# Attention and mixture of experts on one core: head parity of q and K on alternate partitions, W1 from tile 2 on

## The chip, the cores and the metric

The kernel runs on one core of a Trainium2 chip. The metric is the device time of one execution in microseconds. A profile of one execution comes with the runs; its times are read from the start of its span.

## What is computed

Eight batches of 576 tokens with eight heads of 64 go through attention in chunks of 64 tokens; the result, 4608 rows of 512, goes through a layer of eight experts. Each row either skips the layer or goes to the one expert with the highest logit.

```python
scores = scale * np.matmul(q_c, k_c.transpose(0, 1, 2, 4, 3))      # chunks of 64
scores = scores - np.max(scores, axis=-1, keepdims=True)
attn = np.exp(scores); attn = attn / (attn.sum(-1, keepdims=True) + 1e-09)
x = heads_to_rows(np.matmul(attn, v_c))                            # 4608 x 512
do_compute = x @ w_skip > 0
e_idx, gate_w = argmax and softmax weight of x @ w_gate
h = np.maximum(x @ w1[e], 0.0)                                     # 512 -> 1024
out = x + do_compute * gate_w * (h @ w2[e])                        # 1024 -> 512
```

## The kernel before

**Two parts.** The first part walks over 36 tiles of 128 tokens (two chunks) and does the attention, the router's logits and, spread over the tiles, the routing. The second part takes the experts one after the other in an order found at run time, gathers the rows of each, and multiplies them with W1 (`hp`, L483) and W2 (`sp`, L508). The order of the instructions on each engine is the order in which the Python code writes them.

**A tile of the first part.** Four loads bring it in: q (one transfer, L133), K (two, L136) and v (one, L141), all on SP's queue. A tile of q or K has 128 rows of 512 floats: the contraction index, head dimension by parity of the head, lies on the partitions, so two heads share a tile of 128 partitions. K's tile `kbd` is twice as wide, with the heads of parity 0 in the left half on one half of the partitions and those of parity 1 in the right half on the other; the rest is zero. One matmul so gives the scores of two heads apart (`pe_scores`, L240). There are six K tiles, filled with zeros once at the start (L147) and used in turn. The first of K's transfers goes to partitions 0 to 63, the second to 64 to 127.

Then come, each on its engine: the copy of the scores out of PSUM on ACT (`sc`, L245), the row maximum on DVE (L250), its subtraction on POOL (L255), the exponential on ACT (`px`, L259), the transpose on PE (L266) and its copy on ACT (`ps`, L271), the product with v on PE (L279), the division on DVE (`x`, L292), another transpose (L307) and the split into two float16 halves (L312, L317) for the logits (L324). The loop in line 675 runs these for neighbouring tiles in one iteration: scores of tile i, exponential and transpose of tile i-1, the product with v of tile i-2, and so on. Tile i+5's q and K and tile i+4's v are asked for in iteration i.

**The first expert's weights.** Beside the tiles the weights of the expert that comes first are loaded and split into float16 halves, in 16 pieces: eight of W1, then eight of W2. `W_AT` lists the tile at which each piece is asked for (`load_piece`, L351). Near the end of an iteration one piece may be converted: `conv_w1` (L357 on ACT, L358 on DVE) for W1, `scale_w2` and `conv_w2` (L362, L363 on ACT, L367 on POOL) for W2, when the tile number is at least two above the piece's entry in `W_AT` (L710, L712). The pieces share four buffers `wst`. On ACT a conversion so stands between the `ps` copy of one tile and the `sc` copy of the next.

**Stores.** The x of a tile is stored by SP (L301), from tile `X_FROM` on one a tile, towards the end three. Gathers of rows for the first expert (POOL, L227) read them back, the first ones late in the first part.

**The start.** DVE fills the first two K tiles, POOL the other four, each half tile by itself; then DVE makes the constants `ones` and `zeros`, with which PE runs ten warm-up matmuls (L171) ahead of the first scores.

Of the kernel before, what the change touches and what calls it, by code (L numbers as in the profile page):

```python
# [18 lines left out]
P = 128  # L19
B, H, S, D = 8, 8, 576, 64  # L20
CH = 64
NTOK = B * S
NT = NTOK // P
DM = H * D
NE = 8
FF = 1024
KC = DM // P
FC = FF // P
# [8 lines left out]
WSETS = 3  # L37
PACE, PACE1 = 2800.0, 1500.0
QB, KB, VB, AHEAD, VAHEAD = 6, 6, 6, 5, 4
W_AT = tuple(range(1, 9)) + tuple(range(10, 34, 3))  # L40
X_FROM = 9
XB = 14
TLEAD = 2
LLEAD = 1
# [34 lines left out]
def constants():  # L79
    c, r = np.zeros((P, CCOLS), np.float32), np.zeros((1, RCOLS), np.float32)  # L80

    def put(name, a):
        lo, hi = (_C if name in _C else _R)[name]
        (c if name in _C else r)[:, lo:hi] = np.asarray(a, np.float32).reshape(-1, hi - lo)

    put("ident", np.eye(P))
    put("upper", np.triu(np.ones((P, P)), 1))
    put("wdesc", np.arange(NE, -1, -1))
    put("cbase", np.tile([*(np.arange(NE) * RS), NE * RS - RS // 2], GS[0]))
    put("cb8", -RS * np.arange(NE))  # L90
    put("last", np.arange(P)[:, None] * np.ones(P) == P - 1)
    put("tri", np.tril(np.ones((NE, NE))))
    put("kbase", np.arange(NE)[::-1] - NE * RS * np.arange(NE) + (1 << 19) * (np.arange(NE) == FIRST))
    put("eio", np.arange(NE))
    put("eio2", np.repeat(np.arange(NE), NE))
    put("caps", np.repeat([sum(b) for b in BLOCKS], NE))
    put("jthr", P * np.arange(NJ))
    put("siota", np.arange(NJ))
    tok = np.arange(NT)[None, :] * P + np.arange(P)[:, None]
    put("tok", tok)  # L100
    put("tlo", tok % TB + 1)
    put("thi", tok // TB)
    put("iota", np.arange(P))
    put("cell", RS * np.arange(NE)[:, None] + P * np.arange(NB)[None, :])
    return c, r
# [3 lines left out]
def moe_attention_kernel(ctx: ExitStack, tc: tile.TileContext, qk: bass.AP, vv: bass.AP, cst: bass.AP, crow: bass.AP, wall: bass.AP, out: bass.AP):  # L109
    nc = tc.nc  # L110
# [15 lines left out]
    T = [dict() for _ in range(NT)]  # L126
    halves = (slice(0, CH), slice(CH, P))
    kbd = [ap.tile([P, 2, DM], F32, name=f"k{i}", bufs=1) for i in range(KB)]

    def load_qk(t):  # L130
        if t < NT:
            T[t]["q"] = ap.tile([P, DM], F32, name="q", bufs=QB)
            nc.sync.dma_start(T[t]["q"], qk[t, 0])  # L133
            T[t]["k"] = kbd[t % KB]
            for a, r in enumerate(halves):
                nc.sync.dma_start(T[t]["k"][r, a], qk[t, 1, r])  # L136

    def load_v(t):
        if t < NT:
            T[t]["v"] = ap.tile([P, 2, KC, VW], F32, name="v", bufs=VB)  # L140
            nc.sync.dma_start(T[t]["v"], vv[t])  # L141
# [1 line left out]
    man = tc.manual_schedule()  # L143
    man.__enter__()
    for i, k in enumerate(kbd):
        for a, r in enumerate(halves):
            (nc.vector if i < 2 else nc.gpsimd).memset(k[r, 1 - a], 0.0)  # L147
    csb = cpool.tile([P, CCOLS], F32, name="csb")
    rsb = cpool.tile([1, RCOLS], F32, name="rsb")
    load_qk(0)  # L150
    nc.sync.dma_start(csb, cst)
    load_qk(1)
# [40 lines left out]
    def more_constants():  # L193
        w = C("wsg").rearrange("p (k n) -> p k n", k=KC)
        nc.vector.tensor_scalar(wsg[:, :, 0], w, SW, None, op0=ALU.mult)
        nc.vector.scalar_tensor_tensor(wsg[:, :, 1], w, SW, wsg[:, :, 0], op0=ALU.mult, op1=ALU.subtract)

        nc.vector.tensor_copy(iota, C("iota").unsqueeze(2).to_broadcast([P, P, G]))

    def route_constants():  # L200
        nc.gpsimd.tensor_copy(upper, C("upper"))
        nc.gpsimd.tensor_copy(cbase, C("cbase"))
        nc.gpsimd.tensor_copy(recs[:, :, 0], C("tok"))
        nc.gpsimd.tensor_copy(rvs[:, :, 0], C("tlo"))
        nc.gpsimd.tensor_copy(rvs[:, :, 1], C("thi"))
# [92 lines left out]
    def store_x(n):  # L298
        for _ in range(min(n, len(xq))):
            t, x = xq.pop(0)  # L300
            nc.sync.dma_start(out[t * P:(t + 1) * P, :], x)  # L301
# [28 lines left out]
    def route_step():  # L330
        c = next(routes[0][1], None)
        if c is None:
            done_g.append(routes.pop(0)[0])
        paused[0] = c is LATE
        return c or 0.0

    def route_late():
        if paused[0]:
            route_step()

    cws, cw2, stw, done1 = [], [], [None], [0]

    def load_piece(m):
        kind, f = m // FC, m % FC
        r = slice(kind * P * KC, (kind + 1) * P * KC)
        if not kind or f % 2 == 0:
            while len(cws) + len(cw2) // 2 >= STB:
                conv_w1()
            stw[0] = stpool.tile([P, CW], F32, name="wst")
        st = stw[0][:, DM * (kind * f % 2):][:, :DM]  # L350
        nc.sync.dma_start(st, wall[FIRST, f, :, r])  # L351
        (cw2 if kind else cws).append((st, wsets[0][:, 0, f, r], wsets[0][:, 1, f, r]))

    def conv_w1():
        st, hi, lo = cws.pop(0)
        done1[0] += 1
        nc.scalar.activation(hi, st, AF.Copy, scale=SW)  # L357
        nc.vector.scalar_tensor_tensor(lo, st, SW, hi, op0=ALU.mult, op1=ALU.subtract)  # L358
# [253 lines left out]
    def on(f, t):  # L612
        if 0 <= t < NT:
            f(t)
# [32 lines left out]
    scaled, done2 = [0], [0]  # L647

    def more_w2(n):
        for m in range(done2[0], min(FC, done2[0] + n)):  # L650
            while scaled[0] <= m:
                scale_w2(scaled[0])
                scaled[0] += 1
            conv_w2(m)
        done2[0] += n
# [3 lines left out]
    def see(i):  # L659
        while seen[0] < len(EARLY) and len(done_g) >= EARLY[seen[0]]:  # L660
            m = seen[0]
            evq.append((i, early_rec, m))
            seen[0] += 1

    def event(i, e):
        evq.remove(e)
        _, f, m = e
        f(m)
        if f is early_rec:
            evq.insert(0, (i + 1, early_gather, m))  # L670
        elif f is early_gather and m < FIRST_UNIT:
            evq.append((i + 3, early_xt, m))
        return 0.0 if f is early_gather else 0.5

    for i in range(NT):
        load_qk(i + AHEAD)
        on(pe_scores, i)
        on(ac_scores, i)
        if i == 0:
            more_constants()  # L680
        opened = paused[0]
        route_late()
        on(ac_exp, i - 1)
        on(ve_max, i)
        on(po_sub, i)
        if i == 2:
            route_constants()
        load_v(i + VAHEAD)
        on(pe_pv, i - 2)
        on(ac_rr, i - 2)  # L690
        on(ve_norm, i - 2)
        store_x(0 if i < X_FROM else 1 if i <= NT - AHEAD else 3)
        if i in W_AT:
            load_piece(W_AT.index(i))
        on(pe_xtrans, i - 3)
        on(ac_hi, i - 3)
        on(ve_lo, i - 3)
        on(pe_logits, i - 4)
        on(pe_ptrans, i - 1)
        on(ac_ptrans, i - 1)  # L700
        used = 0.0
        see(i)
        due = [e for e in evq if e[0] <= i and not (opened and e[1] is early_xt)]
        if due:
            used += event(i, due[0])
        while routes and used < SLOT:
            used += abs(route_step())
            if paused[0]:
                break
        if cws and i >= W_AT[done1[0]] + 2:  # L710
            conv_w1()
        elif scaled[0] < len(cw2) and i >= W_AT[FC + scaled[0]] + 2:  # L712
            more_w2(1)
    while cws:
        conv_w1()
# [1 line left out]
    a, b = NT - 2, NT - 1  # L717
# [204 lines left out]
def lay_out(q, k, v, moe_w_skip, moe_w_gate, moe_w1, moe_w2):  # L922
    nch = S // CH

    def cols(a):
        a = a.reshape(B, KC, 2, nch, CH, D).transpose(0, 3, 2, 5, 1, 4)
        return a.reshape(NT, 2, 2, D, KC, CH).transpose(0, 2, 3, 1, 4, 5).reshape(NT, P, DM)

    qk = np.ascontiguousarray(np.stack([cols(q), cols(k)], axis=1))
    vv = np.ones((NT, P, 2, KC, VW), np.float32)  # L930
    vv[..., :D] = v.reshape(B, KC, 2, nch, CH, D).transpose(0, 3, 2, 4, 1, 5).reshape(NT, 2, P, KC, D).transpose(0, 2, 1, 3, 4)
    cst, crow = constants()
    wsg = np.concatenate([moe_w_skip[:, None], moe_w_gate], axis=1)
    lo, hi = _C["wsg"]
    cst[:, lo:hi] = wsg.reshape(KC, P, NE + 1).transpose(1, 0, 2).reshape(P, -1)
    w1 = moe_w1.reshape(NE, KC, P, FC, P).transpose(0, 3, 2, 1, 4).reshape(NE, FC, P, KC * P)
    w2 = moe_w2.reshape(NE, FC, P, DM)
    wall = np.ascontiguousarray(np.concatenate([w1, w2], axis=3))
    return {"in_qk": qk, "in_vv": vv.reshape(NT, P, VC), "in_cst": cst, "in_crow": crow, "in_wall": wall}
# [14 lines left out]
```

## Time and profile before

| | |
|---|---|
| median of 3 runs | 371.21 us (370.55 to 376.26) |
| profiled execution | 373.6 us, span 371.8 us |
| busy share of the span | PE 88%, weight loads 63%, DVE 68%, ACT 51%, POOL 31% |
| moved by DMA | 81.82 MB, mean 220 GB/s |
| granted clock of TensorE | 0.975 in the mean |

The profile's page gives busy times of each engine, busy tenths in 40 equal slices of the span, the DMA queues, the chain of work that ended last, and the costliest groups of instructions. A row of a group or of the timeline names the engine, the line, the operation, what it writes and reads by the program's names, and in brackets how long the engine had been idle and what ended that. In the views by windows a row has the window and its length, busy time (and count) of PE, weight loads, DVE, ACT and POOL, the granted clock, the share of time in which DMA engines were busy (it can be a little above 1, as packets overlap) and the rate in GB/s. A row on a transfer ends with its size and the median time from issue to landing in us. SPq is the queue of SyncE, which issues the loads and stores of the first part.

### The profile page before, as it was taken

To read this page: it belongs to the slowest core of one execution; us is meant where nothing else is said; L and a number is where in the kernel's file an instruction comes from. 1 tells how busy PE (TensorE), PEld (TensorE's weight loads), DVE (VectorE), ACT (ScalarE), POOL (GpSimd) and SP (SyncE) were. 2 spreads that over 40 slices of the span, in tenths; PEclk is the share of its full clock that TensorE was granted. 3 is DMA by queue.
4 is the path that set the end of the run, shared out by engine and by line. 5 is a ranking of instruction groups with operands and counts; after the bars stand their busy time and mean duration, and the time that the engine had idled before them with its cause. 6 is when DMAs were issued, how large, how long until landed. Compare 5 with 4: busy or idle time off the path is not lost.

```text
span 371.8 us, 9893 instructions
## 1 busy us (share of the span) xinstructions
PE 327.6 (88%) x3900; PEld 235.0 (63%) x3900; DVE 252.7 (68%) x474; ACT 191.0 (51%) x360; POOL 113.9 (31%) x121
## 2 busy tenths in 40 slices
PE   5739777989879988769999999999999999999991
PEld 2527666867758777555774555575664856769580
DVE  6427656877667778579787895695786777956120
ACT  1527667768766888410374573374453553644020
POOL 8413222434342544023423042621424113011111
PEclk9987999989998999999999999999999999999997
DMA  7999999999999996115585758755866686551000
GB/s 223 261 272 258 249 248 300 314 336 307 309 309 310 298 360 239 70 31 183 205 332 168 271 168 288 258 181 184 282 227 210 203 281 204 168 189 27 29 24 26
DMA packets 34979, 81.82 MB, mean 220 GB/s; under 512 B 4831, under 2 KB 4832, under 8 KB 34930
## 3 DMA queue, kind: packets, MB, share of 16 engines
q1 hardware_dynamic: 31826, 71.83, 63.9%
q0 software_dynamic: 3104, 9.33, 7.1%
q8 instruction: 32, 0.52, 0.6%
q14 instruction: 17, 0.14, 0.1%
HBM read 67.11 MB, written 14.17 MB: 219 GB/s over the span
## 4 chain that ended last, share of the span: by engine, by line
PE 50%; DVE 3%; DMA 1%; ACT 1%; issue 1%; POOLq 0%; DVEq 0%; ACTq 0%
PE sp L508 25%; PE hp L483 22%; PE xt L472 2%; DMA wst<-in_wall 1%; DVE wset L224 1%; ACT wset L223 1%; DVE ht L488 1%; DVE bv L439 0%; PE spq L483 0%; ACT ht L487 0%; POOLq L950 0%; DVE one L431 0%; PE rk L443 0%; DVE x L292 0%; DVE xs L317 0%
## 5 line engine op out<-in xcount | busy, mean ns | idle before, releaser
L508 PE MATMUL sp<-wset,ht 128*128 128x512 f16 (+7 forms) x552 | 102.5, 379 | 0.0
L483 PE MATMUL hp<-xt,wset 128*128 128x288 f16 (+7 forms) x828 | 93.4, 273 | 1.4 <-DVE ht L488 1.3
L483 PEld LDWEIGHTS <-wset 128*128 128x128 f16 x864 | 78.2, 98 | 21.4 <-issue 5.4
L508 PEld LDWEIGHTS <-ht 128*128 128x128 f16 (+7 forms) x552 | 45.7, 101 | 45.5 <-issue 2.1
L224 DVE SCALAR_TENSOR_TENSOR wset<-wst,wset 128x1024 f16<-128x1024 f32 x56 | 67.5, 1218 | 6.7 <-ACT wset L223 6.5
L223 ACT ACTIVATE wset<-wst 128x1024 f16<-128x1024 f32 x56 | 58.0, 1050 | 2.8 <-DMA wst<-in_wall 2.7
L487 ACT ACTIVATE ht<-hp 128x288 f16<-128x288 f32 (+7 forms) x69 | 26.4, 384 | 62.9 <-PE hp L483 61.7
L255 POOL TENSOR_TENSOR sc<-sc,mx 128x512 f32<-128x512 f32 x36 | 37.6, 1044 | 64.9 <-DVE mx L250 63.9
L227 POOL DMA_INDIRECT out<-ys,sidx x18 | 21.4, 1190 | 105.9 <-DVE ys L520 91.2
L488 DVE SCALAR_TENSOR_TENSOR ht<-hp,ht 128x288 f16<-128x288 f32 (+7 forms) x69 | 28.3, 420 | 22.7 <-ACT ht L487 21.9
L240 PE MATMUL spq<-k,q 128*64 128x128 f32 x576 | 42.0, 291 | 0.7 <-ACT sc L245 0.7
L266 PE MATMUL pt<-csb,px 128*128 128x128 f32 x144 | 23.9, 290 | 20.5 <-ACT px L259 20.2
L250 DVE TENSOR_REDUCE mx<-sc 128x8 f32<-128x512 f32 x36 | 24.6, 684 | 23.5 <-ACT sc L245 23.4
L240 PEld LDWEIGHTS spq<-k,q 128*64 128x64 f32 x576 | 32.9, 144 | 7.8 <-issue 4.7
L473 ACT ACTIVATE xt<-xt 128x512 f16<-128x512 f32 (+7 forms) x20 | 10.1, 512 | 43.5 <-PE xt L472 37.0
L245 ACT ACTIVATE sc<-spq 128x512 f32<-128x512 f32 x36 | 21.2, 590 | 17.0 <-PE spq L240 16.5
L266 PEld LDWEIGHTS pt<-csb,px 128*128 128x128 f32 x144 | 15.4, 143 | 22.9 <-ACT px L259 22.8
L317 DVE SCALAR_TENSOR_TENSOR xs<-xp,xs 128x512 f16<-128x512 f32 x36 | 24.6, 683 | 4.0 <-ACT xs L312 3.9
L292 DVE TENSOR_TENSOR x<-o,rr 128x512 f32<-128x512 f32 x36 | 24.9, 692 | 3.5
L279 PE MATMUL o<-v,ps 64*64 64x65 f32 x1152 | 26.4, 232 | 0.7 <-ACT ps L271 0.7
L271 ACT ACTIVATE ps<-pt 128x512 f32<-128x512 f32 x36 | 21.5, 598 | 9.6 <-PE pt L266 8.5
L227 POOL DMA_INDIRECT xg<-out,sidx x18 | 23.4, 1302 | 7.7 <-issue 4.3
(124 smaller groups left out, 333.1 us busy)
## 6 DMA issues: line engine op xcount, KB each, us to landing
wst<-in_wall SPq DMA_DIRECT2D x56, 512.0 KB, 4.1
v<-in_vv SPq DMA_DIRECT2D x36, 260.0 KB, 5.2
q<-in_qk SPq DMA_DIRECT2D x36, 256.0 KB, 5.8
k<-in_qk SPq DMA_DIRECT2D x72, 128.0 KB, 5.5
out<-x SPq DMA_DIRECT2D x36, 256.0 KB, 5.2
wst<-in_wall SPq DMA_DIRECT2D x16, 256.0 KB, 6.6
csb<-in_cst SPq DMA_DIRECT2D x1, 348.5 KB
xg<-out,sidx POOLq DMA_INDIRECT x18, 4.9
```

The lines of the kernel that those rows point to most:

```text
L223: nc.scalar.activation(w[:, 0, fc, :], st, AF.Copy, scale=SW)
L224: nc.vector.scalar_tensor_tensor(w[:, 1, fc, :], st, SW, w[:, 0, fc, :], op0=ALU.mult, op1=ALU.subtract)
L227: ins = nc.gpsimd.indirect_dma_start(**kw)
L240: nc.tensor.matmul(sp[halves[c], 2 * j:2 * j + 2, :], q[:, c, j, :], k[:, c, j], start=True, stop=True, skip_group_check=True)
L255: nc.gpsimd.tensor_tensor(sc, sc, T[t].pop("mx").unsqueeze(2).to_broadcast([P, H, CH]), op=ALU.subtract)
L266: nc.tensor.transpose(pt[:, j, :], px[:, j * P:(j + 1) * P], ident)
L279: nc.tensor.matmul(o[halves[c], a, j * VW:(j + 1) * VW], pt[halves[a], j, halves[c]], v[halves[a], c, j, :], start=True, stop=True, skip_g ...
L292: nc.vector.tensor_tensor(x.rearrange("p (j a d) -> p a j d", j=KC, a=2), o[:, :, :, :D], rr.to_broadcast([P, 2, KC, D]), op=ALU.mult)
L483: nc.tensor.matmul(hp, w()[:, a, fc, j * P:(j + 1) * P], xt[:, b, j, :n], start=(m == 0), stop=(m == 11))
L487: nc.scalar.activation(ht[:, 0, fc, :n], hp, AF.Relu)
L488: nc.vector.scalar_tensor_tensor(ht[:, 1, fc, :n], hp, 0.0, ht[:, 0, fc, :n], op0=ALU.max, op1=ALU.subtract)
L508: nc.tensor.matmul(y[c * P // cg:c * P // cg + n], ht[:, a, fc, o:o + n], w[:, b, fc, P * KC:], start=(f == 0 and m == 0), stop=(f == fw - ...
```

## The change

The layout of q and K in memory is changed by the host: the row of a tile is now head dimension times two plus parity of the head, where it was parity times 64 plus head dimension. K's two transfers each take one parity: every second row of the source, to every second partition of the K tile. A K tile is filled with zeros by one instruction over all of it, three tiles by DVE and three by POOL; the transfers now overlap with what was filled and so wait for it. The score matmuls are written as before, their contraction running over the same values in another order. W1's pieces are asked for at tiles 2 to 9 in place of 1 to 8, W2's where they were; each piece is converted from three tiles behind its entry on, in place of two; x is stored from tile 10 on, in place of 9. Behind the fills all lines of the changed kernel have numbers smaller by one.

```diff
-W_AT = tuple(range(1, 9)) + tuple(range(10, 34, 3))
-X_FROM = 9
+W_AT = tuple(range(2, 10)) + tuple(range(10, 34, 3))
+X_FROM = 10
...
             T[t]["k"] = kbd[t % KB]
-            for a, r in enumerate(halves):
-                nc.sync.dma_start(T[t]["k"][r, a], qk[t, 1, r])
+            for a in range(2):
+                nc.sync.dma_start(T[t]["k"].rearrange("(d h) a f -> h d a f", h=2)[a, :, a], qk[t, 1].rearrange("(d h) f -> h d f", h=2)[a])
...
     for i, k in enumerate(kbd):
-        for a, r in enumerate(halves):
-            (nc.vector if i < 2 else nc.gpsimd).memset(k[r, 1 - a], 0.0)
+        (nc.vector if i < 3 else nc.gpsimd).memset(k, 0.0)
...
-        if cws and i >= W_AT[done1[0]] + 2:
+        if cws and i >= W_AT[done1[0]] + 3:
             conv_w1()
-        elif scaled[0] < len(cw2) and i >= W_AT[FC + scaled[0]] + 2:
+        elif scaled[0] < len(cw2) and i >= W_AT[FC + scaled[0]] + 3:
             more_w2(1)
...
     def cols(a):
-        a = a.reshape(B, KC, 2, nch, CH, D).transpose(0, 3, 2, 5, 1, 4)
-        return a.reshape(NT, 2, 2, D, KC, CH).transpose(0, 2, 3, 1, 4, 5).reshape(NT, P, DM)
+        a = a.reshape(B, KC, 2, nch, CH, D).transpose(0, 3, 5, 2, 1, 4)
+        return a.reshape(NT, 2, D, 2, KC, CH).transpose(0, 2, 3, 1, 4, 5).reshape(NT, P, DM)
```

## The prediction

> **What bounds the kernel now.** I read the page's slices first, to see which stretch is short of what, then the chain that ended last, then the tile cadence on PE, the waits on ACT, and the DMA rate in short windows.
>
> ```profile
> PE   5739777989879988769999999999999999999991
> DMA  7999999999999996115585758755866686551000
> ```
>
> A slice is 9.3 us. In the first fifteen the DMA engines are never free while PE is not full; from slice 17 on it is the other way round. The change touches only the first part, the attention tiles. The chain that ended last begins where that part ends, with the last tile's x:
>
> ```profile
> 154.59 0.70 DVE x L292
> ```
>
> Everything behind it is one unbroken chain from there, so a tile loop that ends earlier moves the end of the program by as much. How fast are the tiles? The PE rows of the score matmuls (L240), one row a tile, give it (the first here is tile 4, that at 58.15 tile 12, the last tile 35):
>
> ```profile
> 19.14 1.09 PE L240 MATMUL spq<-k,q 128*64 128x128 f32 x16
> 29.16 1.98 PE L240 MATMUL spq<-k,q 128*64 128x128 f32 x16
> 41.14 1.09 PE L240 MATMUL spq<-k,q 128*64 128x128 f32 x16
> 45.50 1.09 PE L240 MATMUL spq<-k,q 128*64 128x128 f32 x16
> 58.15 1.09 PE L240 MATMUL spq<-k,q 128*64 128x128 f32 x16
> 66.07 1.09 PE L240 MATMUL spq<-k,q 128*64 128x128 f32 x16
> 68.98 1.09 PE L240 MATMUL spq<-k,q 128*64 128x128 f32 x16
> 76.64 1.75 PE L240 MATMUL spq<-k,q 128*64 128x128 f32 x16
> 81.10 1.09 PE L240 MATMUL spq<-k,q 128*64 128x128 f32 x16
> 84.71 1.09 PE L240 MATMUL spq<-k,q 128*64 128x128 f32 x16
> 144.02 1.09 PE L240 MATMUL spq<-k,q 128*64 128x128 f32 x16
> ```
>
> A tile that waits for nothing takes 2.91 us (66.07 to 68.98): scores, copy, exp, transpose, the next scores, hand to hand between PE and ACT. Tile 4 takes 10.02 us, tile 8 4.36. What holds them is on ACT: the conversion of W1 (L357) stands ahead of the next tile's score copy and waits for its load.
>
> ```profile
> 26.43 0.63 ACT L357 ACTIVATE wset<-wst 128x512 f16<-128x512 f32 x1 [6.53 <-DMA wst<-in_wall]
> 41.31 0.60 ACT L271 ACTIVATE ps<-pt 128x512 f32<-128x512 f32 x1 [0.25 <-PE pt L266]
> 42.99 0.63 ACT L357 ACTIVATE wset<-wst 128x512 f16<-128x512 f32 x1 [1.09 <-DMA wst<-in_wall]
> ```
>
> ```profile
> ACT wset L357 <- DMA wst<-in_wall: 12.2, 7, 6.5
> ACT wset L362 <- DMA wst<-in_wall: 5.8, 5, 2.1
> ```
>
> These two rows, W1 and W2, are 18.0 us, and nothing else on ACT or PE in the tile loop waits on a transfer for long. Why are the loads late? The windows (last two columns: DMA share, GB/s) show the rate going up and down within each tile of the early part, with the engines busy all the time:
>
> ```profile
> 14.10:14.90 0.80, 0.80 (x38) 0.60 (x34) 0.00 (x0) 0.47 (x1) 0.00 (x0) 1.00 1.06 377
> 15.00:16.90 1.90, 1.31 (x20) 1.14 (x20) 1.49 (x3) 1.21 (x4) 1.07 (x2) 1.00 1.06 210
> 30.00:50.00 20.00, 16.09 (x318) 13.37 (x316) 12.54 (x24) 13.59 (x29) 4.52 (x5) 0.94 1.07 256
> 60.00:120.00 60.00, 52.26 (x1023) 44.14 (x1023) 42.90 (x98) 42.92 (x91) 23.36 (x25) 0.94 1.02 312
> 134.60:136.60 2.00, 2.00 (x53) 1.81 (x50) 1.29 (x6) 1.75 (x4) 0.83 (x2) 1.00 1.05 375
> ```
>
> The last window is the telling one. SP issued the last K here:
>
> ```profile
> 129.31 1.42 SPq L136 DMA_DIRECT2D k<-in_qk  x2
> ```
>
> K takes 5.5 us from issue to landing (row below), so by 134.6 no K is left; v, W2 and x are, and they run at 375 GB/s. With K in the stream the same kinds make 256 to 312. That is the case for K's two half transfers being the slow ones, with what queues behind them.
>
> **The change part by part.** First the rate. Sizes:
>
> ```profile
> wst<-in_wall SPq DMA_DIRECT2D x16, 256.0 KB, 6.6
> v<-in_vv SPq DMA_DIRECT2D x36, 260.0 KB, 5.2
> q<-in_qk SPq DMA_DIRECT2D x36, 256.0 KB, 5.8
> k<-in_qk SPq DMA_DIRECT2D x72, 128.0 KB, 5.5
> ```
>
> A tile with a W1 piece moves 256 + 2 x 128 + 260 + 256 KB = 1.053 MB: 4.11 us at 256 GB/s, which is the cadence seen, and 2.79 us at 377. The engines need 2.91 plus what the conversion adds: the copy at 41.31 ends at 41.91, the conversion would end 0.63 later at 42.54, and the scores end at 41.14 + 1.09 = 42.23, so 0.3: 3.2 us. A later tile moves the same with x for W1, and a third of a W2 piece: 1.140 MB, 3.65 us at 312, 3.02 at 377. The engines there took 144.02 - 58.15 = 85.87 us for 23 tiles; without the 5.8 us of waits and 1.3 us of slow clock (below) 3.42 each. So the rate decides: at 312 and below DMA sets the cadence, at 377 the engines do.
>
> What will K's rate be? No row shows a transfer to every second partition. Bounds: as slow as now, or as q (377 GB/s, the window in which q and its like move). I take near q: the new transfers have the same rows of 2 KB, the same 64 of them, the same count of DMAs; what differs is where they land, and full spread over the partitions is what q, W and v have, which run fast whenever K is absent. The 134.60 window also holds a W2 piece, whose source rows too are 2 KB out of every 4 KB, as K's will be; 375 there speaks against a price for the strided source.
>
> [...]
>
> Second, W1. Loads go from tiles 1–8 to 2–9 and conversions from two tiles behind to three. On SP (wst is the weight tile, DMAHW0 to 7 the eight landing semaphores that turn by turn hold a new DMA until the eighth before it has landed) the first W1 stood here before, behind tile 6's loads:
>
> ```order
> L133 DMA q_205<-in_qk 128x512 [waits DMAHW1_49,PE_49]
> L136 DMA k0_82<-in_qk 64x512 [waits DMAHW2_49]
> L136 DMA k0_82<-in_qk 64x512 [waits DMAHW3_49]
> L141 DMA v_224<-in_vv 128x520 [waits DMAHW4_49]
> L351 DMA wst_226<-in_wall 128x512 [waits DMAHW5_49]
> ```
>
> It has left that place, and comes first here, behind tile 7's:
>
> ```order
> L133 DMA q_227<-in_qk 128x512 [waits DMAHW5_49,PE_49]
> L136 DMA k1_83<-in_qk 64x512 [waits DMAHW6_49]
> L136 DMA k1_83<-in_qk 64x512 [waits DMAHW7_49]
> L141 DMA v_251<-in_vv 128x520 [waits DMAHW0_49,PE_49]
> L350 DMA wst_275<-in_wall 128x512 [waits DMAHW1_49]
> ```
>
> So a q, two K and a v have moved ahead of it. On ACT (ps is the copy of the transposed scores, sc of the next tile's scores) its conversion stood between the two, before:
>
> ```order
> L312 ACTIVATE xs<-xp 128x512 [waits PE_49]
> L271 ACTIVATE ps<-pt 128x512 [waits PE_49,Activation_49]
> L357 ACTIVATE wset<-wst 128x512 [waits DMAHW5_49]
> L245 ACTIVATE sc<-spq 128x512 [waits PE_49,Activation_49]
> L259 ACTIVATE px<-sc 128x512 [waits Pool_49]
> ```
>
> In the same place now the score copy follows at once:
>
> ```order
> L311 ACTIVATE xs<-xp 128x512 [waits PE_49]
> L270 ACTIVATE ps<-pt 128x512 [waits PE_49,Activation_49]
> L244 ACTIVATE sc<-spq 128x512 [waits PE_49,Activation_49]
> L258 ACTIVATE px<-sc 128x512 [waits Pool_49]
> L284 ACTIVATE rr<-o 128x8 [waits DVE_49,PE_49]
> ```
>
> The conversion comes two tiles further down. The load on SP, and the v one tile later:
>
> ```profile
> 19.57 0.33 SPq L351 DMA_DIRECT2D wst<-in_wall  x1
> 23.35 0.33 SPq L141 DMA_DIRECT2D v<-in_vv  x1
> ```
>
> The first conversion was due at 26.43 - 6.53 = 19.90; it is now due two tiles later, 25.8. Its load was issued at 19.57 and landed at 26.4. At the old rate it would now go out behind the v of 23.35, about a microsecond sooner since no W is ahead, 22.4, and land near 29: a wait of 3 us. At 377 the 33 DMAs ahead of it and its own bytes (8 tiles of q and K, 7 of v, 0.36 MB of constants, 0.26 of W: 6.7 MB) take 17.8 us from the first issue on, with start and landing some 21: no wait. So I take the W1 row off whole, 12.2. For W2 the same load gets a tile more and a cadence that no longer lags: 5.8 off, but DMA's 3.02 lies above the 2.91 of the shortest tiles, so I leave 1.3 of it.
>
> Third, the clock, which drops after the idle stretches:
>
> ```profile
> 25.70:32.50 6.80, 4.38 (x54) 3.60 (x55) 3.93 (x7) 4.63 (x10) 1.04 (x1) 0.50 1.06 276
> 76.90:80.30 3.40, 3.40 (x52) 2.89 (x49) 3.03 (x7) 1.72 (x4) 0.96 (x2) 0.50 1.05 319
> ```
>
> Tile 17 (76.64) took 4.46 us where tile 18 took 3.61: 0.85; tile 5 (29.16 to 33.58) 4.42, less 0.47 of wait and 3.2: 0.75. A third, shorter one I put at 0.4. Without the waits that go ahead of them, 2.0 off.
>
> Fourth, the start. One fill of 128x1024 replaces two of 64x512, three tiles on DVE in place of two:
>
> ```profile
> 1.19 1.19 SPq L136 DMA_DIRECT2D k<-in_qk  x2
> 0.90 2.38 DVE L147 MEMSET k<- 64x512 f32 x4 [0.90 <-PEq L947]
> 3.84 4.43 PE L171 MATMUL rk<-zeros,ones 128*128 128x512 f16 x10 [3.84 <-DVE zeros L165]
> 5.91 3.18 DVE L195 TENSOR_SCALAR wsg<-csb 128x36 f16<-128x36 f32 x1 [2.12 <-DMA csb<-in_cst]
> ```
>
> ```profile
> L147 DVE MEMSET k<- x4: 485/485/485, 0.9 to 2.8; 64x512 f32 x4
> ```
>
> The four took 0.485 each with gaps of 0.15. Three of the same length would end 0.6 earlier, three of twice the length 0.8 later; a fill's time should go with its elements per partition, so 0.7. The warm-up matmuls stand behind DVE's fills and tile 0's scores behind them: 0.7 us on the path. K's loads now also wait for their fill, and on SP the constants and all later loads queue behind the first K: it goes out at about 1.9 instead of 1.2. That is hidden: csb, behind K, had landed by 5.91, and the warm-up ends at 8.27. POOL's three fills are no more work than its eight.
>
> The sum: -12.2 - 5.8 + 1.3 - 2.0 + 0.7 = -18.0 us. It is made in the profiled execution, 373.6 us with a span of 371.8, so 355.6; the median of the runs is 371.2, 2.4 below that execution, so **353.2**.
>
> **The rivals.** [...]
>
> [...]
>
> *K gains half*: cadence (4.11 + 2.79) / 2 = 3.45 with W1, 0.25 above the engines for 8 tiles, 3.34 later, under 3.42: 2 to 3 us of the waits stay, 356.
>
> *K gets slower*, because rows alternate in source and target. In the 60:120 window K's own share is 3.65 us less the other 0.878 MB at 377 (2.33): 1.3 us a tile, 200 GB/s. [...] Against: the W2 piece in the fast window.
>
> *Gathers wait for stores*: stores start a tile later, and POOL's first gather of x needs the store of tile 16.
>
> ```profile
> 112.55 0.35 SPq L301 DMA_DIRECT2D out<-x  x1
> 127.01 1.22 POOL L227 DMA_INDIRECT xg<-out,idx  x1 [0.17 <-DMA k<-in_qk]
> ```
>
> That store went out 14.5 us ahead; a tile less is 11, over the 5 it takes to land. If SP falls two tiles behind it costs POOL and the next subtraction 2 us: 355, within the range.
>
> **How the numbers follow.** Forecast 0.68, half gain 0.14, K as slow as now 0.11, K slower 0.05, the gather's wait 0.02. The predicted time is the forecast's, 353.2. The range reaches down to 348 (all waits gone, no cost at the start: -20, and 3 more for stalls of PE behind late copies that are not in the two rows) and up to 366, the case of K unchanged. 2% of 371.2, about what a measurement can tell from no change, is 7.4 us, so faster means under 363.8: forecast, half gain and gather, 0.84, less what could go wrong in each of them, 0.80. Within 2%: 0.14; slower: 0.06.
>
> **What would show it.** Right: the window 30:50 at 320 GB/s or more; the row of L356 on ACT (the old L357) under 2 us in total; L361 under 2; PE at full clock from 9 us to the end of the tiles; tile 35's scores near 126 instead of 144; tile 0 at 8.9. Wrong: DMA share at 1 and 256 GB/s in the early window as before, with waits of 1 us still ahead of each conversion; or waits of PE for q or K, which would mean that the lead of the loads is used up instead.

## The result, and the profile after the change

The change takes 360.77 us in the median of four runs (358.74 to 362.97), where the kernel before, run beside it, takes 372.27 (370.55 to 376.26): a ratio of 0.971, 95% interval 0.962 to 0.979. It is faster by 2 to 4%. The prediction was 353.2 us, its range 348 to 366: the median lies in the range, 7.6 us above the forecast. In two of the experiments below one execution stands far from the others of its kernel (540.08 and 1792.32 us) and is left out. The profiled execution took 362.97 us with a span of 361.2, so 10.6 of span less where 18.0 were forecast. Behind the fills every line number is one lower than before (L240 is L239 now).

The page's slices, PE and DMA:

```profile
PE   4799988798996988789989999999999999999991
DMA  6999999999999962146586586774777587551000
```

The early gaps of PE are closed (the third slice stood at 3 before), and DMA falls off a slice earlier. The start of the score matmuls, one row a tile: tiles 0, 4, 5, 12, 31, 32 and 35, and behind them tile 31 of the kernel before.

```profile
8.70 1.09 PE L239 MATMUL spq<-k,q 128*64 128x128 f32 x16
...
19.44 1.09 PE L239 MATMUL spq<-k,q 128*64 128x128 f32 x16
22.40 1.09 PE L239 MATMUL spq<-k,q 128*64 128x128 f32 x16
...
44.89 1.09 PE L239 MATMUL spq<-k,q 128*64 128x128 f32 x16
...
113.08 1.09 PE L239 MATMUL spq<-k,q 128*64 128x128 f32 x16
...
120.64 1.28 PE L239 MATMUL spq<-k,q 128*64 128x128 f32 x16
...
130.98 1.09 PE L239 MATMUL spq<-k,q 128*64 128x128 f32 x16
```

```profile
129.09 1.09 PE L240 MATMUL spq<-k,q 128*64 128x128 f32 x16
```

Tile 4 takes 2.96 us in place of 10.02. Tile 12 starts at 44.89 in place of 58.15, but tile 35 only at 130.98: from tile 12 to tile 35 it takes 86.1 us, as before (85.9). The early part has gained all that there is to see; what the later part gained went somewhere. Tile 31 alone takes 7.56 us (113.08 to 120.64).

The windows (busy times, then granted clock, DMA share, GB/s) and the waits (sum, count, longest, us):

```profile
30.00:50.00 20.00, 17.94 (x360) 14.80 (x353) 17.12 (x36) 16.70 (x38) 6.26 (x6) 1.00 0.95 312
60.00:120.00 60.00, 51.73 (x1064) 43.87 (x1062) 46.03 (x102) 43.52 (x93) 26.18 (x26) 0.98 0.99 337
```

```profile
POOL xg L226 <- DMA k<-in_qk: 3.2, 1, 3.2
...
ACT wset L356 <- DMA wst<-in_wall: 2.3, 4, 0.7
ACT wset L361 <- DMA wst<-in_wall: 2.2, 3, 1.0
```

312 GB/s for 256, 337 for 312; the waits of W1 fell from 12.2 to 2.3, those of W2 from 5.8 to 2.2. The first row is new: POOL's first gather of x, a wait that was 0.2 before. The chain of work behind the tile loop:

```profile
142.26 0.70 DVE x L291
...
156.31 2.50 PE hp L482 x12
...
177.94 5.65 DMA wst<-in_wall
```

From tile 35's scores to the end it is 230.2 us, where it was 227.8. Two of these pieces were shorter before, the matmuls at full clock:

```profile
168.28 1.31 PE hp L483 x12
...
188.72 5.13 DMA wst<-in_wall
```

By stretches of the span, in us (forecast: the prediction's terms put where they fall):

| stretch | before | after | measured | forecast |
|---|---|---|---|---|
| start to tile 12's scores | 58.15 | 44.89 | -13.3 | -12.2 W1, -0.75 clock, +0.7 start: -12.3 |
| tile 12 to tile 31 | 70.94 | 68.19 | -2.8 | -4.5 W2, -1.25 clock: -5.8 |
| tile 31 to tile 35 | 14.93 | 17.90 | +3.0 | 0 |
| tile 35 to the end | 227.8 | 230.2 | +2.4 | 0 |

So two things are to be settled: whether the target of K's transfers made the early gain, and what the gather waits for.

### The profile page after: what moved, and what is told of

The parts are those of the page before. It is cut to its first block, busy times and chain, and to the rows that moved or that the text cites. A ratio compares the mean times of both kernels' runs of the same rounds, so it can differ in the third digit from the quotient of the medians.

```text
span 361.2 us, 9889 instructions
## 1 busy us (share of the span) xinstructions
PE 325.4 (90%) x3900; PEld 233.1 (65%) x3900; DVE 252.4 (70%) x473; ACT 190.2 (53%) x360; POOL 112.4 (31%) x116
## 4 chain that ended last, share of the span: by engine, by line
PE 52%; DVE 3%; ACT 2%; DMA 2%; issue 1%; POOL 0%; POOLq 0%; DVEq 0%; ACTq 0%
PE sp L507 26%; PE hp L482 23%; PE xt L471 2%; DMA wst<-in_wall 2%; ACT wset L222 1%; DVE wset L223 1%; ACT ht L486 1%; DVE bv L438 0%; PE spq L482 0%; PE rk L442 0%; DVE ht L487 0%; POOL out L226 0%; DVE one L430 0%; DVE x L291 0%; DVE xs L316 0%
## 5 line engine op out<-in xcount | busy, mean ns | idle before, releaser
L482 PE MATMUL hp<-xt,wset 128*128 128x288 f16 (+7 forms) x828 | 94.8, 275 | 1.4 <-DVE ht L487 1.3
L239 PE MATMUL spq<-k,q 128*64 128x128 f32 x576 | 39.6, 280 | 0.7 <-ACT sc L244 0.7
L239 PEld LDWEIGHTS spq<-k,q 128*64 128x64 f32 x576 | 30.9, 137 | 7.4 <-issue 4.7
L278 PE MATMUL o<-v,ps 64*64 64x65 f32 x1152 | 25.4, 226 | 0.7 <-ACT ps L270 0.7
L306 PE MATMUL xp<-csb,x 128*128 128x128 f32 x144 | 24.2, 291 | 1.2 <-issue 0.7
```

Of the source, the lines that this page charges most:

```text
L239: nc.tensor.matmul(sp[halves[c], 2 * j:2 * j + 2, :], q[:, c, j, :], k[:, c, j], start=True, stop=True, skip_group_check=True)
L278: nc.tensor.matmul(o[halves[c], a, j * VW:(j + 1) * VW], pt[halves[a], j, halves[c]], v[halves[a], c, j, :], start=True, stop=True, skip_g ...
L482: nc.tensor.matmul(hp, w()[:, a, fc, j * P:(j + 1) * P], xt[:, b, j, :n], start=(m == 0), stop=(m == 11))
```

## The experiments

Ratios are to the kernel before, run on the same chip, each with its 95% interval.

### K alone, and W alone

K's side alone (layout, fills, transfers); the edit is against the change:

```diff
-W_AT = tuple(range(2, 10)) + tuple(range(10, 34, 3))
-X_FROM = 10
+W_AT = tuple(range(1, 9)) + tuple(range(10, 34, 3))
+X_FROM = 9
...
-        if cws and i >= W_AT[done1[0]] + 3:
+        if cws and i >= W_AT[done1[0]] + 2:
...
-        elif scaled[0] < len(cw2) and i >= W_AT[FC + scaled[0]] + 3:
+        elif scaled[0] < len(cw2) and i >= W_AT[FC + scaled[0]] + 2:
```

> The new layout, fills and K transfers alone; W1 from tile 1, conversions two tiles behind, stores from tile 9, as before the change. Theory (the pattern of K's target sets the rate): 30:50 moves at 310 GB/s or more in place of 256, the conversions of W1 still wait some 5 us, since each load has a tile less than with the change, and the gather in tile 31 waits less, since stores go out a tile earlier: 359 to 364 us. Rival (the later W carries the gain): 256 GB/s in 30:50, 369 us or more.

Measured: 363.39 us, ratio 0.981 (0.970 to 0.991). The gather did not wait less, as expected, but 4.7 us; more on this below.

```profile
30.00:50.00 20.00, 19.39 (x421) 16.43 (x424) 17.00 (x32) 17.31 (x39) 6.39 (x7) 1.00 0.94 309
```

W alone is the same edit the other way round, on the kernel before.

> The old layout, fills and K transfers; W1 from tile 2, conversions three tiles behind, stores from tile 10, as with the change. Theory: 30:50 stays at about 256 GB/s, W1 still waits 6 us or more: 364 to 369 us. Rival: W1 waits under 3 us and 361 us, as with the whole change.

Measured: 368.56 us, ratio 0.993 (0.989 to 0.997). Its window:

```profile
30.00:50.00 20.00, 16.39 (x288) 13.56 (x292) 13.42 (x25) 13.64 (x30) 5.22 (x5) 0.86 1.06 269
```

Both times came as the theory had them: K alone takes off 7.8 us of 371.2 and W alone 2.6, together 10.4; the whole change took off 11.5. The rate follows K: 309 GB/s with the new transfers, 269 without.

### Target or source

The change alters two things about a K transfer: it reads every second row, and writes every second partition. The first kernel keeps the new target and reads 64 rows in one piece:

```diff
-                nc.sync.dma_start(T[t]["k"].rearrange("(d h) a f -> h d a f", h=2)[a, :, a], qk[t, 1].rearrange("(d h) f -> h d f", h=2)[a])
+                nc.sync.dma_start(T[t]["k"].rearrange("(d h) a f -> h d a f", h=2)[a, :, a], qk[t, 1, halves[a]])
```

(K is laid out in memory as before, q as with the change.)

> The change with K alone laid out in memory as before, so that each of K's transfers reads 64 rows in one piece and spreads them over every second partition. Theory (the target decides): a packet of K stays near 84 ns, 30:50 at 310 GB/s, 361 us. Rival (reading every second row is what helps): K slow, 256 to 270 GB/s, 365 to 369 us.

Measured: 362.28 us, ratio 0.973 (0.961 to 0.984).

```profile
30.00:50.00 20.00, 17.43 (x352) 14.51 (x351) 16.91 (x38) 17.21 (x38) 6.25 (x6) 1.00 0.97 326
```

The second is the opposite cross:

```diff
-                nc.sync.dma_start(T[t]["k"].rearrange("(d h) a f -> h d a f", h=2)[a, :, a], qk[t, 1].rearrange("(d h) f -> h d f", h=2)[a])
+                nc.sync.dma_start(T[t]["k"][halves[a], a], qk[t, 1].rearrange("(d h) f -> h d f", h=2)[a])
```

> The change with the opposite cross: each of K's transfers reads every second row, and puts the 64 rows on one half of the partitions, as before the change (q is laid out to match). Theory: K slow as before, 256 to 270 GB/s in 30:50, 365 to 369 us. Rival (the source decides): 310 GB/s, 361 us.

Measured: 370.25 us, ratio 0.999 (0.995 to 1.003). Its window and its waits:

```profile
30.00:50.00 20.00, 16.10 (x310) 13.38 (x311) 13.35 (x25) 13.64 (x30) 5.21 (x5) 0.91 1.03 279
```

```profile
ACT wset L356 <- DMA wst<-in_wall: 8.0, 8, 2.8
...
ACT wset L361 <- DMA wst<-in_wall: 5.6, 4, 2.7
```

It is the target. With the same lead of W and the same fills, the halves as target cost everything that the change gives: 13.6 us of waits for W are back. The missed part is the size: 365 to 369 were expected, and it is no faster than before at all. The packets say the same. By the records the median packet of 2 KB between 30 and 50 us took 119 ns before, 122 with W alone and 100 in this kernel, but 84 in the change and in both other kernels with the new target.

### The rates by themselves

A kernel without any of the computation: nine stages of 16 loads of 256 KB each in pieces of 2 KB, one stage after the other, on SP's queue but for the eighth. The places of two stages:

```python
h = slice(i % 2 * 64, i % 2 * 64 + 64)
nc.sync.dma_start(b[h, i // 2], src[i // 2, :, h].rearrange("c p f -> p c f"))               # stage 2
nc.sync.dma_start(b[32:96, i], src[i, :, 32:96].rearrange("c p f -> p c f"))                 # stage 7
```

> No attention at all: nine stages of 16 loads of 256 KB each, one stage after the other, all in pieces of 2 KB, then the output written from one of the buffers. Stages: 1 all 128 partitions; 2 partitions 0-63 and 64-127 by turns; 3 every second partition from every second row, by turns; 4 every second partition from 64 rows in one piece; 5 halves of the partitions from every second row; 6 always 0-63; 7 always 32-95; 8 the halves by turns on two queues at once; 9 as 1. [...] Rival (a transfer with 64 rows is slow by itself): 2 to 8 all near 210.

A window from the middle of each stage, in their order (the last three columns: granted clock, DMA share, GB/s):

```profile
22.00:29.00 7.00, 0.00 (x0) 0.00 (x0) 1.00 0.99 344
38.00:46.00 8.00, 0.00 (x0) 0.00 (x0) 1.00 1.05 302
55.00:62.00 7.00, 0.00 (x0) 0.00 (x0) 1.00 0.94 300
71.00:78.00 7.00, 0.00 (x0) 0.00 (x0) 1.00 0.94 335
87.00:97.00 10.00, 0.00 (x0) 0.00 (x0) 1.00 1.07 231
108.00:120.00 12.00, 0.00 (x0) 0.00 (x0) 1.00 1.07 201
130.50:137.50 7.00, 0.00 (x0) 0.00 (x0) 1.00 1.00 336
147.00:155.00 8.00, 0.00 (x0) 0.00 (x0) 1.00 1.07 278
164.00:169.00 5.00, 0.00 (x0) 0.00 (x0) 1.00 0.98 321
```

Read the share beside the rate, and the packets beside both. By the records of this run a packet of 2 KB takes 84 ns in the median in stages 1, 3, 4, 7 and 9, but 104 in stage 2, 151 in stage 5, 171 in stage 6 and 138 in stage 8. Stages 1, 3, 4, 7 and 9 reach 300 to 344 GB/s at a share of 1.00 or less; their windows hold pauses (in stage 3 a transfer lands at 57.32, 1.55 us behind the one before, where 0.67 is usual). A later window of stage 3, under one of stage 2, shows the two patterns without them:

```profile
43.00:48.00 5.00, 0.00 (x0) 0.00 (x0) 1.00 1.05 299
60.50:64.50 4.00, 0.00 (x0) 0.00 (x0) 1.00 1.02 378
```

Stages 2, 5, 6 and 8 are over 1.04 and yet slower: the engines are busy with packets that take longer. Always 0 to 63 (stage 6) is 201, and 64 other neighbours, 32 to 95 (stage 7), are at 336, near all 128 (344 and 321). So 64 rows are not slow by themselves, and neither are neighbours; those on 0 to 63 are. (Always 64 to 127 was not run.) Halves by turns (stage 2) are at 302, not the 210 expected; why was not shown. With rows read two apart the halves fell to 231 (stage 5), for which I have no reason; in the attention kernel no such loss shows (279 GB/s with halves read two apart, 269 with W alone). Two queues (stage 8) gain nothing over one: 278 beside 302.

### What the gather waits for

POOL around the first gather of x in the change:

```profile
109.75 1.04 POOL L254 TENSOR_TENSOR sc<-sc,mx 128x512 f32<-128x512 f32 x1
113.94 1.21 POOL L226 DMA_INDIRECT xg<-out,idx  x1 [3.15 <-DMA k<-in_qk]
115.19 1.05 POOL L254 TENSOR_TENSOR sc<-sc,mx 128x512 f32<-128x512 f32 x1
```

The subtraction at 115.19 stands behind the gather; tile 31's exponential waits for it (1.40 us), and so PE. The row names K, but the gather doesn't need K. What it needs are the stores of tiles 0 to 16, the last of them issued at 104.62 and landed at 109.1, before POOL was free. The rows on DMA queues have another candidate, a packet of an instruction queue shortly ahead of it (kind, packets, MB, share; window 111.5 to 112.5):

```profile
q14 instruction: 1, 0.01, 1.9%
```

It came at 111.92, 2.0 us before the gather started; in the runs with K alone, the new target and the old target the same packet came 2.0 to 2.3 us before a gather that waited 4.7, 3.5 and 4.1 us. These kernels share with the change that POOL has three K fills at the start where it had eight. My guess was a piece of POOL's code that comes late.

Stores earlier:

```diff
-X_FROM = 10
+X_FROM = 8
```

> The change with stores from tile 8 in place of 10, two tiles ahead of the gather's need. Theory A (POOL's code): the gather still waits 3 us or more, 360 to 362 us. Rival B (the store): the wait is gone, 356 to 359 us.

Measured: 361.87 us, ratio 0.975 (0.970 to 0.981).

```profile
116.26 1.26 POOL L226 DMA_INDIRECT xg<-out,idx  x1 [4.21 <-DMA out<-x]
```

The stores fall: tile 16's had landed by 103.6, yet the wait is longer, and the packet again came 2.0 us ahead of it (114.23).

More instructions on POOL, five at the start:

```diff
+    pad = cpool.tile([P, 5], F32, name="pad")
+    for i in range(5):
+        nc.gpsimd.memset(pad[:, i:i + 1], 0.0)
```

> The change with five more fills of 128x1 on POOL at the start, which nobody reads, so that POOL has as many instructions ahead of its first gather as before the change (68 in place of 73 in the records without them). Theory A (the gather in tile 31 waits for POOL's code: in four kernels a packet of an instruction queue comes 2.0 to 2.3 us before it, each time with 68 instructions of POOL behind it): its wait of 3.2 us is gone, tile 31 takes under 5.5 us in place of 7.6, 356 to 359 us. Rival B (it waits for the store of tile 16 or for the loads around it): the wait stays at 3 us or more, 361 us.

Measured: 358.67 to 363.82 us in three executions, ratio 0.975 (0.965 to 0.985), the profiled one 359.05 us. The first gather waits for next to nothing, tile 31 takes 5.30 us.

```profile
110.36 1.21 POOL L229 DMA_INDIRECT xg<-out,idx  x1 [0.17 <-issue]
```

The same five behind tile 12's subtraction:

> The change with the five extra fills of 128x1 on POOL put behind tile 12's subtraction, not at the start. If the number of POOL's instructions ahead of the gather decides when its code comes, a packet of the instruction queue comes long before the gather, as in the runs with the fills at the start (at 66 to 70 us), and the gather waits under 0.5 us: 356 to 361 us as the clock falls. Rival (what POOL does at the start, or its length, decides): no packet before the gather, which waits 3 us or more: 360 to 363 us.

Measured: 360.25 us, ratio 0.965 (0.958 to 0.972).

```profile
111.66 1.22 POOL L226 DMA_INDIRECT xg<-out,idx  x1 [0.91 <-DMA k<-in_qk]
```

And the fills split as before, with the new layout:

```diff
-        (nc.vector if i < 3 else nc.gpsimd).memset(k, 0.0)
+        for a in range(2):
+            (nc.vector if i < 2 else nc.gpsimd).memset(k[:, a], 0.0)
```

> The change with the number and split of the fills as before: two K tiles on DVE, four on POOL, each in two instructions (128x512 now), so POOL again has eight fills. If the count of POOL's instructions decides when its code comes, the first gather waits under 0.5 us, tile 31 takes under 5.5 us; and the start: four fills of 0.49 us on DVE in place of three of 0.91, tile 0's scores at 8.2 in place of 8.7. Together 3 to 4 us off the profile of the change where the clock holds: 356 to 359 us. Rival (only instructions that do nothing else helped, or chance): gather waits 3 us, 360 to 362 us.

Measured: 360.22 us (356.30 to 362.27), ratio 0.976 (0.965 to 0.986). Its profiled execution took 356.30 us with a span of 354.5. The median lies in the rival's range, while the wait of the gather went as the theory had it. The gather, then the scores of tiles 0, 31 and 35:

```profile
108.70 1.21 POOL L227 DMA_INDIRECT xg<-out,idx  x1 [0.17 <-DMA out<-x]
```

```profile
7.84 1.34 PE L240 MATMUL spq<-k,q 128*64 128x128 f32 x14
...
110.83 1.09 PE L240 MATMUL spq<-k,q 128*64 128x128 f32 x16
...
125.88 1.09 PE L240 MATMUL spq<-k,q 128*64 128x128 f32 x16
```

With five more instructions on POOL, at the start or behind tile 12, there is no such packet ahead of the gather; one comes at 66 to 69 us instead (77.7 with the extra load below), forty before it, and the wait goes (0.2 to 0.9 us in six kernels with them; 3.2 to 4.7 in the five without). Counted by POOL's records, those of its sequencer included, the packet comes behind the 52nd or 53rd in these six, in the kernel before and with W alone, and behind the 68th or 69th in the five. So in these kernels the count of instructions on POOL decides when the packet comes, and the fewer fills brought it right in front of the gather. That it carries POOL's code is my reading of this alone, as no view names its engine. Why it moves by 45 us for five instructions is not settled. In the profile it costs some 3 us, tile 31 to 35 in 15.1 with half fills beside 17.9; in the medians that does not show, since 360.2 and 360.8 lie within each other's scatter.

### Have the loads anything to spare?

The kernel with half fills, and one more load a tile that nobody reads:

```diff
+            nc.sync.dma_start(ap.tile([P, DM // 2], F32, name="extra", bufs=6), qk[t, 0, :, :DM // 2])
```

> As the run with half fills, and one more load of 128 KB a tile (half the columns of q again, all partitions) into a buffer that nobody reads. If the engines set the cadence of the tile loop now, the loads have some 0.3 us a tile to spare and the loop grows by under 3 us: 357 to 362 us. If DMA still sets it, 36 times 128 KB at 375 GB/s, 12 us, come on top: 368 us or more.

Measured: 378.12 us, ratio 1.025 (1.012 to 1.038).

```profile
143.97 1.09 PE L241 MATMUL spq<-k,q 128*64 128x128 f32 x16
```

```profile
ACT wset L363 <- DMA wst<-in_wall: 7.8, 3, 3.7
ACT wset L358 <- DMA wst<-in_wall: 7.3, 5, 3.4
```

Tile 35 comes 18.1 us later than without, and the waits for W are back. So the stream of loads has nothing to spare. But that the rate of the DMA engines is what it lacks is not shown: 18.1 is more than the 12 expected by the bytes, and the engines were less busy, not more. From 20 to 30 us, with half fills and with the extra load:

```profile
20.00:30.00 10.00, 9.83 (x228) 8.38 (x227) 7.48 (x15) 8.55 (x19) 3.13 (x3) 1.00 0.96 317
20.00:30.00 10.00, 7.61 (x176) 6.44 (x172) 4.52 (x10) 5.49 (x12) 2.08 (x2) 0.97 0.90 288
```

```profile
L140 SPq DMA_DIRECT2D extra<-in_qk x36: 362/584/1447, 4.9 to 137.5; - x36
```

SP issues one load behind the other there, without a pause over 0.2 us from 13.9 to 32.5 (two issues of K, of 1.61 and 1.43 us where 0.56 is usual, are held by something that no row names). An extra load takes 0.58 us of SP in the median, some 21 us in 36 tiles. The first piece of W1 goes out at 24.25 in place of 20.69, and its conversion waits 3.45 us. So a rival that the expectation left out, SP's time to issue, fits the early part better; behind 60 us (share 0.96 for 0.98, 312 GB/s for 331) it is open. Five windows at half clock in its tile loop, none in that of half fills, are part of the 18.1.

### Two versions that should have been faster

The first: the change with the five instructions on POOL, W2 converted two tiles behind its load again, and the warm-up's constants filled right behind the first K tile.

```diff
-        elif scaled[0] < len(cw2) and i >= W_AT[FC + scaled[0]] + 3:
+        elif scaled[0] < len(cw2) and i >= W_AT[FC + scaled[0]] + 2:
```

> Built on the findings: the change, POOL's five fills, W2 converted two tiles behind its load as before (so that the last one no longer stands behind tile 35's scores), and the constants of the warm-up filled behind the first K tile in place of the third. By theory A: 3 to 4 us from the gather, 0.7 from the last W2, and 1 to 2 from a start 2 us earlier, of which waits of W1 may eat half: 354 to 357 us. By B: 358 to 360 us.

Measured: 363.04 us, ratio 0.980 (0.973 to 0.987): a miss. Tile 0 did start at 6.75, but the clock fell to half at 11.3, tile 4 came at 19.4 as in the change, and W2 waited 3.4 us once. The second: half fills, the same early constants, four more warm-up matmuls behind the first scores, the last piece of W2 asked for at tile 30.

```diff
-W_AT = tuple(range(2, 10)) + tuple(range(10, 34, 3))
+W_AT = tuple(range(2, 10)) + tuple(range(10, 31, 3)) + (30,)
...
+        pe_warm((1, 2, 1)[i] if i < 3 else 0)
```

> The version that the findings point to: half fills as in the run beside it, the warm-up's constants right behind the first K tile (tile 0 near 7.2), four more warm-up matmuls in the gaps of PE behind the scores of tiles 0 to 2 so that the clock holds there, and the last piece of W2 asked for a tile earlier so that its scaling stands ahead of tile 35's scores (0.7 us). 353 to 357 us if each holds; 358 or more if the earlier start runs into the loads.

Measured: 357.17 to 362.15 us in five executions, ratio 0.975 (0.963 to 0.987), the profiled one 359.54 us: no better than half fills. Tile 0 started at 6.76 and tile 4 at 18.28, 0.7 ahead of half fills; by tile 12 (44.27 for 44.33) the lead was gone, with W1 waiting 2.1 us on the way. That is the extra load's answer once more: who starts earlier meets the loads.

## Why the prediction came out as it did

The median is in the range, but most of the signs that the prediction named for being right were missed: the rate (312 for 320), the waits for W1 and W2 (2.3 and 2.2 for under 2 each), the clock (one window at half) and tile 35 (130.98 for 126). Of the 7.4 us of span that are short of the forecast, 3.0 lie between tiles 12 and 31, 3.0 between tiles 31 and 35 and 2.4 behind them; the early part gave 1.0 more.

**The rate of K: right.** K near the rate of q was the choice between two bounds; the crosses (326 GB/s with the new target, 279 with halves) and the rates show the target as the cause. In 30:50 the forecast was 320 GB/s or more; the change has 312 at a share of 0.95, half fills 328.

**W1: right, a little too large.** 12.2 were taken off whole, 9.9 went. The early part came out at -13.3 for -12.3 all the same, so some 2 us of it lie in none of the terms.

**W2: right, too large.** 4.5 forecast, 3.6 measured. Between tiles 12 and 31, where the last pieces of W1 now wait 1.0 us as well, the waits for W fell only from 5.3 to 3.2, which is most of what that stretch is short of.

**The start: right.** +0.7 forecast, 8.20 to 8.70 measured, by fills of 0.91 us for 1024 elements a partition, where 512 took 0.485, near what the elements per partition had. Half fills bring it to 7.84, so that this price was not needed.

**The clock: right in kind.** In the tile loop before it was at half for four windows of 3.4 us, in the change for one. The mean granted clock went from 0.975 to 0.984.

**"At 377 the engines do" set the cadence: not shown.** 377 and 375 GB/s came from windows of 0.8 and 2 us. Over 60 us it is 337, and 1.140 MB at that rate are 3.38 us a tile; but such a mean is only the bytes of a tile over its time, whatever sets the pace. The loads by themselves reach 378 (stage 3, the later window). The extra load shows that there was no margin of 0.4 us; the prediction weighed DMA's bytes against the engines and left out SP's time to issue, and which of the two was short is open.

**POOL's fills "are no more work than its eight": the step that failed.** It was true of the time (2.73 us for 4.47) and left out the count. The fewer instructions put a packet of an instruction queue, as I read it POOL's code, in front of the first gather. The rival on the gather had the place and about the size (2 us for 3.2), but the wrong cause, the stores. With the fills split again, tile 35 starts at 125.88, where the prediction had "near 126".

**Behind the tile loop: left out.** The last W2 scaling, now three tiles behind its load, stands behind tile 35's scores: from these to tile 35's x it is 11.28 us (130.98 to 142.26) for 10.57 (144.02 to 154.59); in the first of the two versions above, with W2 two tiles behind its load, it is 10.57 again. One window at half clock now lies on the hand-over (12 matmuls in 2.50 for 1.31), and one load of weights takes 5.65 for 5.13.

**The median as the profile less 2.4: it held, but is no rule.** The profile of the change lies 2.2 above its median, that of half fills 3.9 below (356.30, the lowest of six). One execution stands for the median only to within some 4 us here. So the 355.6 forecast for a profile and the 356.3 measured with half fills look like a proof of the sum, and are not one of the median, which without the gather's wait is still 360.2.

**K as slow as now: mispriced.** The top of the range, 366, was this case, with some 5 us off by W's extra tile alone. No run shows these 5 us: the extra tile gave 2.6 with the old transfers (368.6) and nothing with halves read two rows apart (370.3).

The choice of halves matters: the change and the kernel with halves as target, 360.8 and 370.3 us, differ in nothing else but the layout of q to match.

## What to carry to other kernels

In this case a transfer of half the rows was faster on every second partition (stages 3 and 4, 300 and 335 GB/s) than on 0 to 63 (stage 6, 201), and data laid out so that what goes separately lies on alternate ones took 360.8 us in place of 370.3; try which partitions a transfer fills. A gain where DMA was the bound ends where the next bound begins; count the time to issue the loads beside their bytes and the engines. And an edit that changes the number of instructions on an engine can have a price of its own: here it put a packet of an instruction queue right ahead of a gather, which waited 3.2 to 4.7 us in five kernels; look for such packets ahead of a wait that no data explains.

## What the runs showed of the hardware

In the traces PE's clock falls to half in steps of 3.41 us, in the change both times up to 200 us after a step in which PE was little busy:

```profile
114.25:117.66 3.41, 0.74 (x20) 0.66 (x23) 3.11 (x6) 1.23 (x2) 2.07 (x3) 1.00 0.97 336
117.66:121.08 3.42, 3.42 (x52) 2.90 (x50) 1.68 (x5) 1.04 (x3) 1.96 (x2) 0.50 1.03 392
151.80:155.21 3.41, 1.30 (x14) 0.87 (x12) 3.31 (x8) 0.42 (x2) 0.80 (x2) 1.00 0.00 0
155.21:158.62 3.41, 3.41 (x23) 2.56 (x21) 2.98 (x17) 0.00 (x0) 1.00 (x1) 0.50 0.05 10
```

PE was busy 0.74 and 1.30 us of the 3.41 ahead (third column), and no other step up to 200 us, the first 12 aside, was under 2.0. The other kernels bear this out in part. Their halves came behind steps with 0 to 2.5 us (0.00, 1.01, 1.79 and 0.64 in the kernel before), but the kernel before kept full clock behind one with 1.59 (at 165.7), K alone behind one with 1.49 (at 155.2). So one stall of the change cost another 1.2 us at half clock right behind it (the 12 matmuls above, 2.50 us for 1.31). Where the steps fall differs between the profiled executions (from 0.1 to 2.5 us behind the span's start). That this is the main part of the scatter of 3 us is my estimate; it was not tried.
